# A fused norm, long-convolution and feed-forward kernel: a new model for its static planner, a GpSimd power in the norms, and less combining on TensorE

## The chip, the core and the metric

The kernel runs on one core of a Trainium2 chip. The metric is the device time of one execution in microseconds; lower is better. A core has TensorE (matmuls, "PE" in the profile), VectorE ("DVE"), ScalarE ("ACT"), GpSimd ("POOL") and SyncE ("SP", which here only issues transfers). The program gives each engine its own list of instructions and the semaphores on which it waits for the others.

Times are medians of single executions; a profile shows one execution.

## The reference, cut to what matters

```python
x  = A_q                                        # 2048 rows x 640
h  = x + A(layernorm(x), k, v, shift_k, ssm_k)  # "first norm"; A: kv = shift(k) * v,
                                                #  y = causal FFT convolution of kv with ssm_k, q * y
h2 = h + B(layernorm(h), w_gate, w_up, w_down)  # "second norm"; B: (silu(g) * u) @ w_down, width 1728
# layernorm(x) = (x - mean) / sqrt(var + 1e-5)
```

## The kernel before

The 2048 rows are cut into four blocks of 512 rows. A block's rows lie in four row groups of 128; its 640 columns are worked in two halves. For each block the kernel does: the shift and product k·v (VectorE), forward transforms (TensorE, evicted by ScalarE), products of spectra with those of all earlier blocks (VectorE), inverse transforms (TensorE), the second norm, transposes, and the feed-forward part. The feed-forward matmuls of block j are independent of the convolution of block j+1 and so serve as filler for TensorE while that convolution waits for VectorE and ScalarE.

The order of instructions is not written by hand. The program lists operations with priorities and planned durations. A greedy planner, run when the kernel is built, fixes one order per engine, and the built kernel holds these orders.

```python
# planned durations, us; n = elements per partition
def act_c(n, ptr=False): return 0.17 + 0.000833 * n + (0.09 if ptr else 0)
def dve2(n, psum=False): return 0.15 + 0.00052 * n
def mm_c(n, k=1):        return k * (n / 2400.0 + 0.003)
...
# in the planner: an operation o on engine e, started at t
o.finish = t + o.engs[e]; free[e] = o.finish
for s in o.succ:                                 # hand-off to every consumer: lat = 0.12
    fin = o.finish + (0.0 if o.dma is not None else lat)
...
P.schedule(0.12, dma_model, 1.0)                 # 1.0: when VectorE takes an eviction from ScalarE
```

```python
# both norms end in this; all four row groups at once
if j == 0:      # block 0
    P.op({"act": 0.2}, ... func=ACTF.Sqrt ...)   # square root on ScalarE, then a VectorE reciprocal
else:           # blocks 1 to 3: Newton's method, each o(...) one GpSimd operation on 128x4 numbers
    o(va = src * k1 + eps); o(y = first guess from the bits of va)
    for _ in range(3):
        o(t = y * y); o(t = t * va); o(t = -0.5 * t + 1.5); o(y = t * y)
o(nm = -mean * y)                                # on GpSimd for every block
```

(The two norm snippets are abridged: the arguments of `o` are shown as formulas.)

## Time and profile before

The kernel takes 361.57 us (median of 3, 359.22 to 362.79).

From the page of the kernel before, the span, the busy time of each engine, and two rows of the picture in 40 slices of 9 us (busy tenths of TensorE, and the clock granted to it in tenths):

```profile
span 361.3 us, 5379 instructions
PE 314.9 (87%) x2005; PEld 168.1 (47%) x2024; DVE 225.4 (62%) x366; ACT 203.0 (56%) x319; POOL 68.5 (19%) x147
PE   4697797389999999979999996549999999999993
PEclk9998997559999999999999999558999999999997
```

TensorE is busy 87% of the time, and it is at half clock ("5"; 0.50 in both) in two places: 60-80 us and 227-247 us. Around both it stands again and again.

The table by stage cuts the span at events of the kernel before: start of block 0's feed-forward (75.7), statistics of block 1's second norm ready (140.3), its transposes (152.7), statistics of block 2 (232.9), its transposes (242.9), start of its feed-forward (247.6). Columns: stretch and its length, then the busy time of TensorE, weight loads, VectorE, ScalarE and GpSimd with their counts, granted clock, share of DMA, GB/s.

```profile
core 0: us, PE busy (x) PEld busy (x) DVE busy (x) ACT busy (x) POOL busy (x), PEclk, DMA share, GB/s
0.00:75.70 75.70, 53.50 (x339) 31.57 (x341) 50.26 (x97) 51.14 (x87) 25.08 (x42) 0.87 0.74 244
75.70:140.30 64.60, 63.50 (x398) 31.66 (x403) 50.17 (x79) 43.22 (x66) 12.20 (x24) 0.97 0.30 103
140.30:152.70 12.40, 12.40 (x98) 7.87 (x96) 8.81 (x16) 6.49 (x9) 8.80 (x18) 1.00 0.31 101
152.70:232.90 80.20, 71.83 (x471) 37.26 (x475) 67.94 (x106) 52.47 (x88) 8.92 (x19) 0.96 0.25 85
232.90:242.90 10.00, 3.38 (x23) 1.30 (x22) 6.47 (x13) 6.01 (x11) 6.35 (x15) 0.50 0.19 67
242.90:247.60 4.70, 4.65 (x35) 3.18 (x37) 1.48 (x2) 3.21 (x6) 0.00 (x0) 0.53 0.10 35
```

Between block 2's statistics and its transposes TensorE is busy 3.38 of 10.0 us at half clock (0.50). Between block 1's it is fully busy (12.40 of 12.40 us, clock 1.00).

The GpSimd chain runs from 232.96 to 240.47 us in block 2.

### The profile page before, as it was taken

The numbers are of one execution on the slowest core, as the hardware profiler recorded it, in microseconds if no ns is written. First come the engines' busy times: TensorE is split into PE (matmuls) and PEld (weight loads), VectorE is DVE, ScalarE is ACT, GpSimd is POOL, SyncE is SP. The second block draws the span as 40 slices with busy tenths as digits, with TensorE's granted clock in tenths as the row PEclk, the third lists the DMA queues.
The fourth block names the chain that finished last, engine by engine and source line by source line (L and its number), as shares of the span: only waits on it lengthen the run. The fifth ranks groups of instructions, "written<-read, shape, count | busy, mean of one in ns | idle before, by whom it ended". The sixth has DMA issues, their size and how long they took to land.

```text
span 361.3 us, 5379 instructions
## 1 busy us (share of the span) xinstructions
PE 314.9 (87%) x2005; PEld 168.1 (47%) x2024; DVE 225.4 (62%) x366; ACT 203.0 (56%) x319; POOL 68.5 (19%) x147
## 2 busy tenths in 40 slices
PE   4697797389999999979999996549999999999993
PEld 1374463144435466545445662125444466444561
DVE  1869498486597879578889796955486541122200
ACT  4384988669756745588863257777654503322111
POOL 2504235302502014500240001153100021000000
PEclk9998997559999999999999999558999999999997
DMA  7994558712411531351110135211300101000011
GB/s 224 365 409 148 167 201 214 250 64 109 139 73 43 205 144 39 121 201 36 38 73 2 40 125 164 89 58 37 110 0 10 64 18 38 18 2 0 2 36 37
DMA packets 22013, 37.16 MB, mean 103 GB/s; under 512 B 2616, under 2 KB 17363, under 8 KB 21988
## 3 DMA queue, kind: packets, MB, share of 16 engines
q1 hardware_dynamic: 17524, 20.49, 16.1%
q0 software_dynamic: 3968, 15.98, 13.7%
q10 hardware_dynamic: 496, 0.36, 0.3%
q8 instruction: 16, 0.26, 0.3%
q14 instruction: 9, 0.07, 0.1%
HBM read 22.40 MB, written 2.62 MB: 69 GB/s over the span
## 4 chain that ended last, share of the span: by engine, by line
PE 69%; DMA 9%; ACT 6%; DVE 5%; POOL 5%; issue 4%; ACTq 0%; POOLq 0%; DVEq 0%
PE ps L548 65%; DVE sb L753 4%; PE ps L632 3%; ACT sb L533 3%; DMA sb<-in_B_w_down_dram 2%; PE ps L1067 2%; DMA sb<-in_A_k_dram 2%; DMA sb<-in_A_ssm_k_dram 2%; DMA sb<-in_B_w_gate_dram 2%; ACT sb L894 1%; POOL sb L541 1%; DMA sb<-in_A_v_dram 1%; DMA sb<-in_B_w_up_dram 1%; POOL stt L880 1%; POOL stt L879 1%
## 5 line engine op out<-in xcount | busy, mean ns | idle before, releaser
L548 PE MATMUL ps<-sb 128*128 128x320 bf16 (+3 forms) x1207 | 228.9, 339 | 13.5 <-POOL sb L639 5.1
L753 DVE TENSOR_TENSOR sb<-sb 128x1280 bf16<-128x1280 bf16 (+2 forms) x250 | 161.4, 690 | 44.2 <-ACT sb L533 15.9
L548 PEld LDWEIGHTS ps<-sb 128*128 128x128 bf16 (+2 forms) x1226 | 115.2, 99 | 110.7 <-issue 17.1
L533 ACT ACTIVATE sb<-ps 128x640 bf16<-128x640 f32 (+2 forms) x152 | 106.2, 730 | 91.9 <-PE ps L548 74.0
L548 PE MATMUL ps<-sb,tab 128*64 128x320 bf16 (+2 forms) x622 | 81.2, 326 | 17.4 <-ACT sb L533 11.7
L753 DVE TENSOR_TENSOR sb<-ps,sb 128x1024 bf16<-128x1024 f32 (+3 forms) x44 | 43.9, 1013 | 45.0 <-PE ps L548 39.4
L548 PEld LDWEIGHTS ps<-sb,tab 128*64 128x64 f16 (+2 forms) x622 | 38.2, 105 | 58.9 <-issue 28.0
L1105 ACT ACTIVATE sb<-ps 128x1024 bf16<-128x1024 f32 (+2 forms) x32 | 29.3, 915 | 37.2 <-PE ps L548 37.0
L894 ACT ACTIVATE sb<-sb,stt 128x320 bf16<-128x320 bf16 (+1 forms) x42 | 27.8, 709 | 11.8 <-POOL stt L886 7.5
L536 ACT ACTIVATE sb<-ps 128x640 bf16<-128x640 f32 x24 | 16.5, 702 | 9.4 <-PE ps L548 9.1
L873 POOL TENSOR_SCALAR stt<-stt 128x4 f32<-128x4 f32 x6 | 2.7, 443 | 99.4 <-DVE stt L855 61.1
L632 PE MATMUL ps<-sb 128*128 128x128 bf16 (+1 forms) x96 | 13.2, 233 | 2.5 <-DMA sb<-in_A_ssm_k_dram 2.5
L541 POOL DMA_DIRECT2D sb<-in_A_v_dram x6 | 4.7, 787 | 53.0 <-PE ps L548 53.0
L541 POOL DMA_DIRECT2D sb<-in_A_ssm_k_dram x12 | 7.9, 660 | 33.6 <-PE ps L632 33.5
L851 DVE BATCH_NORM_STATS2 stt<-sb 128x6 f32<-128x320 bf16 x32 | 14.0, 480 | 0.0
L1067 PE MATMUL ps<-sb 128*128 128x128 bf16 x80 | 7.5, 266 | 6.7 <-ACT sb L536 3.5
L913 ACT ACTIVATE sb<-sb,stt 128x640 bf16<-128x640 bf16 x16 | 13.2, 824 | 0.1
L632 PEld LDWEIGHTS ps<-sb 128*128 128x128 bf16 (+1 forms) x96 | 8.6, 117 | 8.3 <-DMA sb<-in_A_ssm_k_dram 3.1
L906 ACT ACTIVATE sb<-sb 128x640 bf16<-128x640 bf16 x16 | 11.8, 734 | 0.1
L534 DVE COPY sb<-ps 128x1280 bf16<-128x1280 bf16 x4 | 3.3, 824 | 12.1 <-PE ps L1067 12.1
L1067 PEld LDWEIGHTS ps<-sb 128*128 128x128 bf16 x80 | 6.4, 122 | 8.6 <-ACT sb L536 4.5
L893 DVE TENSOR_SCALAR sb<-sb,stt 128x640 bf16<-128x640 bf16 x6 | 2.4, 443 | 9.0 <-POOL stt L886 9.0
(30 smaller groups left out, 72.1 us busy)
## 6 DMA issues: line engine op xcount, KB each, us to landing
sb<-sb SPq DMA_DIRECT2D x72, 160.0 KB, 2.2
sb<-in_A_k_dram POOLq DMA_DIRECT2D x6, 560.0 KB, 5.3
out_dram<-sb SPq DMA_DIRECT2D x16, 160.0 KB, 1.8
sb<-cst_den SPq DMA_DIRECT2D x9, 256.0 KB, 5.2
sb<-in_B_w_gate_dram POOLq DMA_DIRECT2D x5, 416.0 KB, 3.6
sb<-in_B_w_up_dram POOLq DMA_DIRECT2D x5, 416.0 KB, 4.2
sb<-in_A_q_dram POOLq DMA_DIRECT2D x3, 640.0 KB, 4.4
sb<-in_A_v_dram POOLq DMA_DIRECT2D x6, 320.0 KB, 4.2
```

The costliest lines, as they stand in the source:

```text
L533: fns = {"act": lambda a: a.activation(out=dst(), in_=src(), func=ACTF.Copy), "dve": lambda v: v.tensor_copy(out=dst(), in_=src())}
L536: fns = {"act": lambda a: a.activation(out=dst(), in_=src(), func=ACTF.Copy, scale=scale), "dve": lambda v: v.tensor_scalar(out=dst(), in0 ...
L541: fns = [(lambda g, d=d, s=s: g.dma_start(d(), s())) for d, s in subs]
L548: return lambda t: t.matmul(o(), l(), r(), start=st, stop=sp)
L632: return t.transpose(B16(pt, b // 2, (b % 2) * CW + d * 128, pr), src, V(IDN, 0, pr, 0, pr))
L753: return lambda v: v.tensor_tensor(out=o(), in0=a(), in1=b_(), op=op)
L851: vec(dve1(CW, False), lambda v: v.bn_stats(st6(l, j, b, c), V(xt, b * D + c * CW, CW)), [(xt, (b, c))], [(ST, ("s", l, j, b, c))], prio, ...
L894: "act": lambda a: a.activation(out=dst(), in_=src(), func=ACTF.Identity, scale=rs(l, j, b), bias=tmv(l, j, 3)[:, b:b + 1])},
L906: P.op({"act": act_c(D) + 0.22}, lambda a, b=b, jt=jt: a.activation(out=V(jt, 0, D), in_=V(xt, b * D, D), func=ACTF.Copy, accum_out=tmv(l, ...
L913: P.op({"act": act_c(D) + 0.3}, lambda a, b=b, jt=jt: a.activation(out=V(jt, 0, D), in_=V(xt, b * D, D), func=ACTF.Square, bias=tmv(l, j, ...
L1067: fns.append(lambda t, k=k, d=d: t.transpose(B16(pt, k, d * 128, 128), V(hn[k], d * 128, 128), V(IDN, 0, 128)))
L1105: P.op({"act": act_c(n)}, lambda a: a.activation(out=dst(), in_=src(), func=ACTF.Silu), rd, wr, -1000, name=f"si{j}{i}")
```

## The change

The intent: plan with durations nearer to the measured ones, and give the plan a TensorE clock that can fall; shorten the norms; take combining work off TensorE where VectorE has time. The diff, cut to its core (the clock rule `pe_end` lowers the planned speed of TensorE by the share of its time that was busy in the plan; its constants, like those of `FRESH`, are planning numbers of the program's):

```diff
+    FRESH = {"pe": 0.22, "act": 0.145, "dve": 0.125, "pool": 0.15, "sp": 0.1}
+    OVERLAP = {"pe": 0.0, "act": 0.105, "dve": 0.085, "pool": 0.0, "sp": 0.0}
...
-                        o.finish = t + o.engs[e]
+                        c = o.engs[e] - self.OVERLAP[e]
+                        o.finish = self.pe_end(t, c) if e == "pe" else t + c
...
-                        fin = o.finish + (0.0 if o.dma is not None else lat)
+                        k = s.deps[o]
+                        if k == 0 or (e == "pe" and "pe" in s.engs):
+                            fin = o.finish
+                        else:
+                            fin = o.finish + max(self.FRESH[x] for x in s.engs)
...
-    RESPE = [True] * 4
+    CMB = [True, False, False, True]      # True: VectorE combines two products before the inverse stage
+    RESPE = [True, True, False, False]    # True: TensorE adds the residual to the feed-forward sum
...
-            return P.op({"pe": mm_c(n, k)}, fns, ...
+            return P.op({"pe": mm_c(n, k) + (0.13 if name.startswith("s2") else 0.03)}, fns, ...
...   # norms: sqrt/reciprocal and the Newton chain are removed
+            vec(0.16, va = src * k1 + eps)
+            P.op({"pool": 0.4}, lambda g: g.tensor_tensor(out=y, in0=va, in1=<-0.5>, op=ALU.pow), ...
+            vec(0.16, nm = -mean * y)
...   # second norm by pairs of row groups
-            (ln_act if LN2A[j] else ln_dve)(1, j, pb + 400)
             for bp in range(2):
+                ln_dve(1, j, pb + 400, range(2 * bp, 2 * bp + 2))
                 ln_bp(j, bp, pb + 400)
...
-        P.schedule(0.12, dma_model, 1.0)
+        P.schedule(dma_model, 0.8)
```

Smaller parts: a GpSimd transfer issue is planned at 0.9 instead of 0.5 us, a freed buffer at 0.14 instead of 0.1 us, one load of block 0 moves from SyncE's queue to ScalarE's. (The lines with `va`, `nm` and `<-0.5>` are abridged.)

More of the change, by code (lines that the diff above doesn't have):

```diff
@@ L42 @@
     ENG = ("pe", "act", "dve", "pool", "sp")
+    FRESH = {"pe": 0.22, "act": 0.145, "dve": 0.125, "pool": 0.15, "sp": 0.1}
+    OVERLAP = {"pe": 0.0, "act": 0.105, "dve": 0.085, "pool": 0.0, "sp": 0.0}
+    WIN = 3.41333
     def __init__(self):
@@ L102, in op, with pe_end, schedule @@
         return o
-    def schedule(self, lat, dma_model, bias):
+    def pe_end(self, t, c):
+        w = self.clock
+        while c > 1e-12:
+            k = int((t + 1.7) // self.WIN)
+            while w["k"] < k:
+                u = w["busy"].get(w["k"], 0.0) / self.WIN
+                if w["s"] == 1.0:
+                    if u < 0.55 and w["k"] > 8:
+                        w["s"] = 0.5
+                elif u >= 0.83:
+                    w["s"] = 1.0
+                w["k"] += 1
+            e = (k + 1) * self.WIN - 1.7
+            if e - t < 1e-9:
+                e += self.WIN
+            d = min(c / w["s"], e - t)
+            w["busy"][k] = w["busy"].get(k, 0.0) + d
+            t += d
+            c -= d * w["s"]
+        return t
+    def schedule(self, dma_model, bias):
+        self.clock = {"k": -1, "s": 1.0, "busy": {}}
         free = {e: 0.0 for e in self.ENG}
@@ L177, in schedule @@
                         if tl.left == 0 and tl.pool is not None:
-                            self.pools[tl.pool].free.append((max(p.finish for p in tl.touch) + 0.1, tl.base, tl.touch))
+                            self.pools[tl.pool].free.append((max(p.finish for p in tl.touch) + 0.14, tl.base, tl.touch))
                     for s in o.succ:
                         s.npred -= 1
-                        fin = o.finish + (0.0 if o.dma is not None else lat)
+                        k = s.deps[o]
[3 more added lines that the diff above has]
+                            fin = o.finish + max(self.FRESH[x] for x in s.engs)
                         s.ready = max(s.ready, fin)
@@ L408, in bass_sequential_preLN__ssm_conv_h3__swiglu_ffn__prompt_kernel @@
     NFB = 14
-    NEWTS = ["pool", "pool"]
-    LN2A = [False, False, False, False]
-    RESPE = [True] * 4
+    CMB = [True, False, False, True]
+    RESPE = [True, True, False, False]
     FM = 1664
@@ L427, in bass_sequential_preLN__ssm_conv_h3__swiglu_ffn__prompt_kernel @@
         tab = es.enter_context(nc.sbuf_tensor("tab", [128, tab_np.shape[1]], f16))
-        stt = es.enter_context(nc.sbuf_tensor("stt", [128, 192 + 32 + 192 + 1], f32))
+        stt = es.enter_context(nc.sbuf_tensor("stt", [128, 192 + 32 + 192 + 8], f32))
         ps = es.enter_context(nc.psum_tensor("ps", [128, 4096], f32))
@@ L541, in dma @@
             fns = [(lambda g, d=d, s=s: g.dma_start(d(), s())) for d, s in subs]
-            return P.op({eng: 0.5 * len(subs)}, fns, reads, writes, prio, after=after, dma=(kb, shuffle), name=name)
+            return P.op({eng: (0.9 if eng == "pool" else 0.5) * len(subs)}, fns, reads, writes, prio, after=after, dma=(kb, shuffle), name=name)
         def pe(fns, n, k, reads, writes, prio, reserve=(), name=""):
-            return P.op({"pe": mm_c(n, k)}, fns, reads, writes, prio, reserve=reserve, name=name)
+            return P.op({"pe": mm_c(n, k) + (0.13 if name.startswith("s2") else 0.03)}, fns, reads, writes, prio, reserve=reserve, name=name)
         def mm(o, l, r, st, sp):
@@ L610, in load_kraw @@
                  (lambda: V(t, 2 * B, B, 0, 64), lambda: dram(A_ssm_k, base + 256 * S, [[S, 64], [1, B]]))],
-                328, [], [(t, 0)], prio, name=f"kraw{j}{c}", eng="pool" if j else ("sp" if c else "act"))
+                328, [], [(t, 0)], prio, name=f"kraw{j}{c}", eng="pool" if j else "act")
         def load_x(j, prio):
@@ L835, in agv @@
             return stt[:, o:o + 8].rearrange("p (b s) -> p b s", b=4)[:, :, 1:2].rearrange("p b s -> p (b s)")
-        def EPS():
-            return stt[:, 416:417]
-        P.op({"pool": 0.1}, lambda g: g.memset(EPS(), LN_EPS), [], [(ST, "eps")], -3000, name="eps")
+        P.op({"pool": 0.1}, lambda g: g.memset(stt[:, 420:424], -0.5), [], [(ST, "half")], -3000, name="half")
         def agm(l, j):
@@ L856, in ln_aggr @@
                 [(ST, ("a", l, j, b))], prio, name=f"ag{l}{j}{b}")
-        def ln_rstd(l, j, prio, two_pass):
-            I32 = dt.int32
-            NEWT = NEWTS[l]
-            va, t, y, nm = (tmv(l, j, i) for i in (0, 1, 2, 3))
-            rd = [(ST, ("ss", l, j, b)) if two_pass else (ST, ("a", l, j, b)) for b in range(4)]
-            c1, c2, c3, c4 = [(ST, ("t", l, j, i)) for i in range(4)]
-            src = va if two_pass else agv(l, j)
-            k1 = 1.0 / D if two_pass else 1.0
-            if j == 0:
-                P.op({"act": 0.2}, lambda a: a.activation(out=t, in_=src, func=ACTF.Sqrt, bias=EPS(), scale=k1), rd + [(ST, "eps")], [c2], prio, name=f"sq{l}")
-                vec(0.16, lambda v: v.reciprocal(out=y, in_=t), [c2], [c3], prio, name=f"rc{l}")
-            else:
-                def o(fn, reads, writes):
-                    P.op({NEWT: 0.3 if NEWT == "pool" else 0.16}, fn, reads, writes, prio, name=f"nr{l}{j}")
-                o(lambda v: v.tensor_scalar(out=va, in0=src, scalar1=k1, scalar2=LN_EPS, op0=ALU.mult, op1=ALU.add), rd, [c1])
-                o(lambda v: v.tensor_scalar(out=y.bitcast(I32), in0=va.bitcast(I32), scalar1=-0.5, scalar2=float(0x5F3759DF), op0=ALU.mult, op1=ALU.add),
-                  [c1], [c3])
-                for _ in range(3):
-                    if NEWT == "pool":
-                        o(lambda v: v.tensor_tensor(out=t, in0=y, in1=y, op=ALU.mult), [c3], [c2])
-                        o(lambda v: v.tensor_tensor(out=t, in0=t, in1=va, op=ALU.mult), [c2, c1], [c2])
-                        o(lambda v: v.tensor_scalar(out=t, in0=t, scalar1=-0.5, scalar2=1.5, op0=ALU.mult, op1=ALU.add), [c2], [c2])
-                        o(lambda v: v.tensor_tensor(out=y, in0=t, in1=y, op=ALU.mult), [c2, c3], [c3])
-                        continue
-                    o(lambda v: v.scalar_tensor_tensor(out=t, in0=y, scalar=-0.5, in1=y, op0=ALU.mult, op1=ALU.mult), [c3], [c2])
-                    o(lambda v: v.tensor_tensor(out=t, in0=t, in1=va, op=ALU.mult), [c2, c1], [c2])
-                    o(lambda v: v.scalar_tensor_tensor(out=y, in0=t, scalar=1.5, in1=y, op0=ALU.add, op1=ALU.mult), [c2, c3], [c3])
-            P.op({NEWT: 0.3 if NEWT == "pool" else 0.16}, lambda v: v.tensor_tensor(out=nm, in0=tmv(l, j, 5), in1=y, op=ALU.mult),
-                 [c3, (ST, ("negm", l, j))], [c4], prio, name=f"nm{l}{j}")
@@ new lines, in ln_rstd @@
+        def ln_rstd(l, j, prio, two_pass, bs):
+            lo, hi = bs[0], bs[-1] + 1
+            va, y, nm, ng = (tmv(l, j, i)[:, lo:hi] for i in (0, 2, 3, 5))
+            if two_pass:
+                src, k1, rd = va, 1.0 / D, [(ST, ("ss", l, j, b)) for b in bs]
+            else:
+                src, k1, rd = agv(l, j)[:, lo:hi], 1.0, [(ST, ("a", l, j, b)) for b in bs]
+            c1, c3, c4 = ([(ST, ("t", l, j, i, b)) for b in bs] for i in (0, 2, 3))
+            vec(0.16, lambda v: v.tensor_scalar(out=va, in0=src, scalar1=k1, scalar2=LN_EPS, op0=ALU.mult, op1=ALU.add), rd, c1, prio, name=f"va{l}{j}")
+            P.op({"pool": 0.4}, lambda g: g.tensor_tensor(out=y, in0=va, in1=stt[:, 420:420 + hi - lo], op=ALU.pow), c1 + [(ST, "half")], c3, prio,
+                 name=f"nr{l}{j}")
+            vec(0.16, lambda v: v.tensor_tensor(out=nm, in0=ng, in1=y, op=ALU.mult), c3 + [(ST, ("negm", l, j, b)) for b in bs], c4, prio,
+                name=f"nm{l}{j}")
@@ L889, in norm @@
         def norm(dst, src, n, l, j, b, reads, writes, prio, name):
-            rd = reads + [(ST, ("negm", l, j)), (ST, ("t", l, j, 2)), (ST, ("t", l, j, 3))]
+            rd = reads + [(ST, ("negm", l, j, b)), (ST, ("t", l, j, 2, b)), (ST, ("t", l, j, 3, b))]
             P.op({"dve": dve4(n), "act": act_c(n) + 0.12}, {
@@ L909, in ln_act @@
             vec(0.16, lambda v: v.tensor_scalar(out=tmv(l, j, 5), in0=tmv(l, j, 4), scalar1=-1.0 / D, scalar2=None, op0=ALU.mult),
-                [(ST, ("sum", l, j, b)) for b in range(4)], [(ST, ("negm", l, j))], prio, name=f"l{l}m{j}")
+                [(ST, ("sum", l, j, b)) for b in range(4)], [(ST, ("negm", l, j, b)) for b in range(4)], prio, name=f"l{l}m{j}")
             for b in range(4):
@@ L914, in ln_act, with ln_dve @@
                     out=V(jt, 0, D), in_=V(xt, b * D, D), func=ACTF.Square, bias=tmv(l, j, 5)[:, b:b + 1], accum_out=tmv(l, j, 0)[:, b:b + 1]),
-                    [(xt, (b, c)) for c in range(2)] + [(ST, ("negm", l, j))], [(jt, 0), (ST, ("ss", l, j, b))], prio, name=f"l{l}v{j}{b}")
-            ln_rstd(l, j, prio, True)
-        def ln_dve(l, j, prio):
-            for b in range(4):
+                    [(xt, (b, c)) for c in range(2)] + [(ST, ("negm", l, j, b))], [(jt, 0), (ST, ("ss", l, j, b))], prio, name=f"l{l}v{j}{b}")
+            ln_rstd(l, j, prio, True, range(4))
+        def ln_dve(l, j, prio, bs):
+            for b in bs:
                 ln_aggr(l, j, b, prio)
-            vec(0.16, lambda v: v.tensor_scalar(out=tmv(l, j, 5), in0=agm(l, j), scalar1=-1.0, scalar2=None, op0=ALU.mult),
-                [(ST, ("a", l, j, b)) for b in range(4)], [(ST, ("negm", l, j))], prio, name=f"l{l}m{j}")
-            ln_rstd(l, j, prio, False)
+            lo, hi = bs[0], bs[-1] + 1
+            vec(0.16, lambda v: v.tensor_scalar(out=tmv(l, j, 5)[:, lo:hi], in0=agm(l, j)[:, lo:hi], scalar1=-1.0, scalar2=None, op0=ALU.mult),
+                [(ST, ("a", l, j, b)) for b in bs], [(ST, ("negm", l, j, b)) for b in bs], prio, name=f"l{l}m{j}")
+            ln_rstd(l, j, prio, False, bs)
         def kv_block(j, c, prio):
@@ L984, in conv_hs @@
             ax = SXt[1, c] if j == 3 else None
+            if CMB[j]:
+                combine((a1, a2), lambda: V2(a1, 0, 640, n, CW), lambda: V2(a2, 0, 640, n, CW), n,
+                        [(a1, i) for i in range(n)], [(a2, i) for i in range(n)], pr, f"{j}{c}{h0}")
             for i, h in enumerate(hs):
@@ L987, in conv_hs @@
                 o_ = i * 640
-                ops_ = [(lambda p0, p1, o_=o_: V(a1, o_, CW, p0, p1), wre), (lambda p0, p1, o_=o_: V(a1, o_ + CW, CW, p0, p1), wneg),
-                        (lambda p0, p1, o_=o_: V(a2, o_, CW, p0, p1), wim), (lambda p0, p1, o_=o_: V(a2, o_ + CW, CW, p0, p1), wim)]
+                if CMB[j]:
+                    ops_ = [(lambda p0, p1, o_=o_: V(a1, o_, CW, p0, p1), wre), (lambda p0, p1, o_=o_: V(a2, o_, CW, p0, p1), wim)]
+                else:
+                    ops_ = [(lambda p0, p1, o_=o_: V(a1, o_, CW, p0, p1), wre), (lambda p0, p1, o_=o_: V(a1, o_ + CW, CW, p0, p1), wneg),
+                            (lambda p0, p1, o_=o_: V(a2, o_, CW, p0, p1), wim), (lambda p0, p1, o_=o_: V(a2, o_ + CW, CW, p0, p1), wim)]
                 cells = [(a1, i), (a2, i)]
@@ L1033, in conv_bp @@
             vec(dve2(2 * CW), tt(hv, hv, lambda: V2(ot, 0, CW, 2, CW), ALU.add), xc2 + [(ot, 0)], xc2, pr, name=f"h{j}{c}{bp}")
-            if not LN2A[j]:
-                for k in range(2):
-                    ln_stats(1, j, bp * 2 + k, c, xt, pr)
+            for k in range(2):
+                ln_stats(1, j, bp * 2 + k, c, xt, pr)
         def conv_c(j, c):
@@ L1192, in dma_model @@
                 dmafree[0] = s + 0.55
-                return s + 2.2
+                return s + 2.3
             s = max(issued + (1.2 if o.eng == "pool" else 0.8), link[0])
```

## The prediction

> **What bounds the kernel now.** The page gives TensorE 314.9 us busy of 361.3 (87%), VectorE 62%, ScalarE 56%; the chain of waits is 69% TensorE. The time is TensorE work at full clock, plus the extra of work at half clock, plus idle. The table of 5-us windows locates the losses. Half clock: 60-80 us (12.6 us busy, about 6 extra) and 227-247 us (10 busy, 5 extra). Idle: the load (8 us before 15 us), 55-80 us (9.5), 215-250 us (12), the tail (6). The two mid-kernel stages lose 16-17 us each; those the change can get. [...]
>
> **Why they stall (timeline by engine).** At 232.9 us block 2's second norm has its statistics; then 15 tiny GpSimd operations (128x4; 0.19 to 0.85 us each) run until 240.5 us: 7.6 us for a reciprocal root. Transposes follow at 242.9; the filler, block 1's feed-forward, is used up by 217. [...] the trace shows one operation at 0.2 us with VectorE idle and 0.8 beside it. In block 0 the reciprocal is ready at 62.5 us, but the last GpSimd multiply waits in its queue behind a w_down transfer until 66.6; transposes begin at 70.9.
>
> **What changes.**
> - The chain becomes VectorE, one GpSimd power, VectorE, by row pairs. Estimate from the 128x4 times: 0.2 + 0.8 + 0.2 us, 1.5 with hand-offs, instead of 7.6. Block 2: 6 us of wait and 1.5 of half clock. Block 0: the multiply leaves the GpSimd queue, but the power is in it behind weight transfers: 0-5 us, I take 3. Blocks 1 and 3 hide under feed-forward matmuls: 0.
> - Square root leaves ScalarE, with one or two table loads of 1.28 us, one in the chain at 39.7 us: 1 us.
> - TensorE: block 3's inverse stage drops 32 of 224 64x320 matmuls (20.2 us in all, so 2.9); residual adds of blocks 2 and 3 drop 16 matmuls of 128x320 (0.151 us each, 2.4). Both lie after 247 us, where TensorE is nearly always busy: 5 us.
> - Added: VectorE combines in block 3 (8 of 0.48 us) and additions for copies at 8 outputs; VectorE is some 55% busy there: nearly free.
> - The new order, from truer latencies: fewer stalls on ScalarE evictions (19 waits, 14.8 us). It is greedy, and VectorE stays over 80% busy from 165 to 240 us: only 3 us.
>
> Sum 5 + 7.5 + 3 + 1 + 3, about 19 us.
>
> **Prediction: 343 us, 8 in 10 between 333 and 354. Faster by over 2%: 0.87; within 2%: 0.11; slower: 0.02.**
>
> **What shows it.** TensorE busy near 300; the stage 225-250 loses under 10 us, and block 2's gap from last statistics to transposes falls from 10 us to about 4; no square root on ScalarE; 55-80 us still has a slow clock, but shorter; block 3's feed-forward, the last 47 us, shrinks by only 1.2.
>
> **What would make it wrong.** The power taking several us; the power stuck behind transfers on the GpSimd queue in block 0 or 2; the new order using up the filler earlier, moving the hole rather than closing it; or the order closing both holes (325-330 us).

(Two passages are cut from it. The one in the first paragraph gave a rule for when the clock falls, and concluded that a stall is paid twice. The traces show the half clock (0.50 in 60-80 and 227-247 us) but not that rule: see "The clock" below. The one in the second paragraph gave a reason why GpSimd is slower beside VectorE; measured are only the durations that follow it (0.2 us with VectorE idle, 0.8 beside it). No term of the sum is cut, it is still about 19 us; the 1.5 us of half clock in block 2's 7.5 were my estimate, which no trace shows apart.)

## More of the kernel before

The timeline of the kernel before (start, duration, engine, line, operation, output<-input, count, and in brackets the idle time before and what ended it):

```profile
140.96 6.17 DVE L753 TENSOR_TENSOR sb<-sb 128x1280 bf16<-128x1280 bf16 x9
150.24 0.80 DVE L893 TENSOR_SCALAR sb<-sb,stt 128x640 bf16<-128x640 bf16 x2 [3.12 <-POOL stt L886]
...
232.96 0.65 POOL L873 TENSOR_SCALAR stt<-stt 128x4 f32<-128x4 f32 x1 [12.23 <-DVE stt L855]
233.69 0.39 POOL L874 TENSOR_SCALAR stt<-stt 128x4 int32<-128x4 int32 x1
...
240.27 0.20 POOL L886 TENSOR_TENSOR stt<-stt 128x4 f32<-128x4 f32 x1
242.87 2.31 PE L1067 MATMUL ps<-sb 128*128 128x128 bf16 x20 [2.78 <-ACT sb L536]
```

## The result and the profile after

The kernel after takes 330.18 us (median of 4, 329.36 to 331.60); the kernel before took 361.88 us in the same rounds. A ratio is the mean time of one kernel's fast runs over that of the other's of the same rounds, so it is not quite the ratio of the medians; here it is 0.914 (95% interval 0.909 to 0.919). The direction was right. The gain is 31.7 us where 19 were predicted, and the time lies just below the range.

From the page of the kernel after:

```profile
span 327.8 us, 5229 instructions
PE 299.1 (91%) x1956; PEld 162.0 (49%) x1976; DVE 235.3 (72%) x406; ACT 197.5 (60%) x310; POOL 47.9 (15%) x67
PE   3899785489999999999999999999989999999992
PEclk9999999579999999999999999999999999999998
```

The half clock is left in one place (0.60 in 54-66 us). Of the 33.5 us between the spans, 15.8 are TensorE busy time (314.9 - 299.1) and 17.7 are TensorE idle time (46.4 before, 28.7 after, each span less busy).

The table by stage of the kernel after, cut at the same events, so that the lines answer to those shown of before:

```profile
0.00:66.30 66.30, 48.88 (x326) 29.77 (x328) 47.39 (x100) 50.94 (x88) 27.82 (x42) 0.93 0.82 268
66.30:122.90 56.60, 55.17 (x352) 27.11 (x358) 49.18 (x78) 40.42 (x60) 7.30 (x10) 0.97 0.37 126
122.90:128.30 5.40, 4.95 (x37) 3.18 (x36) 5.20 (x14) 4.48 (x7) 1.70 (x2) 1.00 0.02 5
128.30:207.30 79.00, 78.51 (x544) 43.23 (x550) 75.50 (x121) 53.95 (x85) 5.69 (x7) 1.00 0.27 91
207.30:212.30 5.00, 4.95 (x39) 2.92 (x38) 4.41 (x15) 3.81 (x6) 1.74 (x2) 1.00 0.28 103
212.30:216.00 3.70, 3.56 (x44) 2.85 (x46) 2.49 (x5) 2.92 (x4) 0.00 (x0) 1.00 0.24 86
```

Line by line the stages shrink by 9.4, 8.0, 7.0, 1.2, 5.0 and 1.0 us; the rest of the kernel, 113.7 us before and 111.8 after, gives 1.9. Two readings matter. The lines that shrink most are those of block 0 and block 1, where I had booked 4 us and nothing. For block 1 this is mostly filler that moved: its two lines hold 15.8 us less TensorE work than before (107 matmuls fewer), the three lines of block 2 hold 98 matmuls more. And block 2's convolution, fourth line, hardly got shorter, but it holds 78.5 us of TensorE work instead of 71.8 and 75.5 us of VectorE work instead of 67.9: the filler now lasts to its end.

The timeline of the kernel after, for the places shown of before:

```profile
123.01 1.70 POOL L894 TENSOR_TENSOR stt<-stt 128x2 f32<-128x2 f32 x2 [2.77 <-DVE stt L932]
124.95 8.68 DVE L783 TENSOR_TENSOR sb<-sb 128x1280 bf16<-128x1280 bf16 x13
...
207.53 1.74 POOL L894 TENSOR_TENSOR stt<-stt 128x2 f32<-128x2 f32 x2 [17.98 <-DVE stt L932]
212.26 1.32 PE L1083 MATMUL ps<-sb 128*128 128x128 bf16 x20
```

Two powers in 1.7 us, with small VectorE operations around them, replace a chain of 7.5 (block 2) and 9.9 us (block 1, 140.26 to 150.20). VectorE no longer stands behind the norm in block 1, and block 2's transposes come with no idle time before them.

### The profile page after: what moved, and what is told of

The parts are those of the page before. It is cut to its first block, busy times and chain, and to the rows that moved or that the text cites. A ratio compares the mean times of both kernels' runs of the same rounds, so it can differ in the third digit from the quotient of the medians.

```text
span 327.8 us, 5229 instructions
## 1 busy us (share of the span) xinstructions
PE 299.1 (91%) x1956; PEld 162.0 (49%) x1976; DVE 235.3 (72%) x406; ACT 197.5 (60%) x310; POOL 47.9 (15%) x67
## 3 DMA queue, kind: packets, MB, share of 16 engines
q1 hardware_dynamic: 17172, 20.16, 17.7%
## 4 chain that ended last, share of the span: by engine, by line
PE 69%; DVE 10%; ACT 8%; DMA 5%; issue 3%; POOL 3%; ACTq 0%; POOLq 0%; DVEq 0%
PE ps L578 65%; DVE sb L783 9%; ACT sb L563 4%; PE ps L662 3%; ACT sb L904 2%; DMA sb<-in_A_ssm_k_dram 2%; DMA sb<-in_A_k_dram 2%; DMA sb<-in_B_w_gate_dram 2%; POOL stt L894 1%; PE ps L1083 1%; POOL sb L571 1%; ACT sb L923 1%; ACT sb L1121 1%; ACT sb L916 1%; DVE stt L878 0%
## 5 line engine op out<-in xcount | busy, mean ns | idle before, releaser
L578 PE MATMUL ps<-sb 128*128 128x320 bf16 (+2 forms) x1192 | 225.0, 338 | 8.3 <-DMA sb<-in_A_shift_k_dram 2.4
L783 DVE TENSOR_TENSOR sb<-sb 128x1280 bf16<-128x1280 bf16 (+2 forms) x258 | 165.6, 683 | 30.1 <-DMA sb<-in_A_k_dram 10.2
L578 PEld LDWEIGHTS ps<-sb 128*128 128x128 bf16 (+3 forms) x1212 | 113.2, 98 | 102.3 <-issue 18.2
L563 ACT ACTIVATE sb<-ps 128x640 bf16<-128x640 f32 (+2 forms) x146 | 101.7, 737 | 44.3 <-PE ps L578 34.9
L783 DVE TENSOR_TENSOR sb<-ps,sb 128x1024 bf16<-128x1024 f32 (+3 forms) x52 | 50.5, 982 | 45.4 <-PE ps L578 42.4
L578 PE MATMUL ps<-sb,tab 128*64 128x320 bf16 (+2 forms) x588 | 70.1, 309 | 7.1 <-DMA sb<-sb 3.0
L578 PEld LDWEIGHTS ps<-sb,tab 128*64 128x64 f16 (+2 forms) x588 | 35.4, 102 | 41.7 <-issue 15.2
L894 POOL TENSOR_TENSOR stt<-stt 128x2 f32<-128x2 f32 (+1 forms) x12 | 12.4, 1039 | 97.2 <-DVE stt L893 76.4
L662 PE MATMUL ps<-sb 128*128 128x128 bf16 (+1 forms) x96 | 13.6, 240 | 2.8 <-DMA sb<-in_A_ssm_k_dram 2.8
L571 POOL DMA_DIRECT2D sb<-in_A_k_dram x6 | 5.9, 987 | 11.7 <-DVE sb L783 11.7
L896 DVE TENSOR_TENSOR stt<-stt 128x2 f32<-128x2 f32 (+1 forms) x12 | 1.9, 160 | 6.8 <-POOL stt L894 6.7
```

Of the source, the lines that this page charges most:

```text
L563: fns = {"act": lambda a: a.activation(out=dst(), in_=src(), func=ACTF.Copy), "dve": lambda v: v.tensor_copy(out=dst(), in_=src())}
L571: fns = [(lambda g, d=d, s=s: g.dma_start(d(), s())) for d, s in subs]
L578: return lambda t: t.matmul(o(), l(), r(), start=st, stop=sp)
L662: return t.transpose(B16(pt, b // 2, (b % 2) * CW + d * 128, pr), src, V(IDN, 0, pr, 0, pr))
L783: return lambda v: v.tensor_tensor(out=o(), in0=a(), in1=b_(), op=op)
L894: P.op({"pool": 0.4}, lambda g: g.tensor_tensor(out=y, in0=va, in1=stt[:, 420:420 + hi - lo], op=ALU.pow), c1 + [(ST, "half")], c3, prio, ...
```

## The experiments

The question is where the 13 us beyond the prediction came from. Theory "operations": the time comes from what was removed (the chain, the square root, TensorE work), and the order is worth little; that is my prediction. Rival "order": the truer plan paces the work, and the operations matter little. "Against after" below is (ratio - 0.914) x 362 us, which takes out the small drift of the kernel before (its medians were 361.4 to 362.8 us on four different chips).

All runs are correct and were timed in 3 rounds:

| run | median us | ratio to before | against after, us |
|---|---|---|---|
| kernel after | 330.2 | 0.914 | 0 |
| order_only | 350.3 | 0.968 | 19.3 |
| ops_only | 356.6 | 0.986 | 25.9 |
| slow_norm | 344.4 | 0.952 | 13.9 |
| before_pow | 359.9 | 0.993 | 28.6 |
| cmb_old | 334.5 | 0.926 | 4.2 |
| no_clock | 335.2 | 0.926 | 4.5 |
| no_overlap | 351.1 | 0.971 | 20.5 |
| no_fresh | 335.9 | 0.931 | 6.1 |
| norm_old | 351.8 | 0.971 | 20.7 |
| scaled_pe | 337.9 | 0.933 | 6.9 |
| wd_late | 331.6 | 0.915 | 0.5 |
| wd_pe104 | 331.3 | 0.915 | 0.2 |
| norm_dve | 341.7 | 0.942 | 10.2 |
| norm1_old | 335.7 | 0.927 | 4.7 |
| norm2_old | 341.9 | 0.944 | 10.6 |
| whole | 334.1 | 0.922 | 2.9 |
| bias10 | 331.3 | 0.915 | 0.5 |
| bias06 | 333.4 | 0.923 | 3.1 |

Half-widths of the 95% intervals are 0.004 to 0.009 of the ratio. The last column compares two such ratios, so its half-width is about 2.4 to 3.7 us (estimate from both intervals); differences below that mean nothing.

### Order alone, operations alone

`order_only` has the planner of after and the operations of before; `ops_only` the reverse.

```diff
# order_only, on the kernel before: FRESH, OVERLAP, pe_end, planned costs and schedule(dma_model, 0.8) as in the change;
#             norms, CMB, RESPE, queues as before
# ops_only, on the kernel after:
-        P.schedule(dma_model, 0.8)
+        P.schedule(0.12, dma_model, 1.0)   # and the old finish, hand-off and cost lines
```

> All operations of the kernel before (long GpSimd chain, residual adds and inverse-stage combines on TensorE), planned with the new latencies and clock rule. Theory 'operations' (the prediction's sum: order worth 3 us): about 355-359 us. Rival theory 'order' (the plan's truer durations pace the feed-forward filler so that block 2's end no longer finds TensorE without work): 336-345 us, and the half-clock stretch at 227-247 us shrinks or is gone.

> All operations of the kernel after, planned with the old latencies and without the clock rule. Theory 'operations': about 345 us (16 of the 19 us predicted). Theory 'order': 348-356 us, with a TensorE hole before block 2's transposes still there.

Alone, the order gains about 12 us (ratio 0.968) and the operations 5 us (0.986). The product of the ratios, 0.954, would be 17 us; together they give 31. Both theories fall: most of the surplus over 17 us exists only when both are there. In `ops_only` the gap before block 2's transposes is still there (TensorE busy 6.0 of 15 us in 225-240 us at a clock of 0.60). In `order_only` it is smaller but there (transposes at 230.1 us, with 3.31 us idle before them). How the two halves combine can be read from the last filler before block 2's transposes: it ended 25.8 us ahead of them in the kernel before, 23.0 in `ops_only`, 9.2 in `order_only`; in the kernel after filler runs right up to them (it ends at 212.21 us, they start at 212.26). The new order makes the filler last longer, the short norm brings the transposes forward, and only both together close the hole.

### The norm in a frozen order

Two runs change only how long the second norm of blocks 1 to 3 takes and leave every order as planned. `slow_norm` puts the old chain into the kernel after, `before_pow` puts the power into the kernel before.

```diff
# slow_norm (after; planned duration stays 0.4, so the order does not move)
-            P.op({"pool": 0.4}, <power>, ...)
+            P.op({"pool": 0.4}, chain if l == 1 and j > 0 and lo == 0 else <power>, ...)   # 13 dependent operations
# before_pow (before; the 13 planned operations keep their places, one is emitted)
+            if j > 0 and l == 1:
+                mine[1].fns = <power>
+                for q in mine[2:]: q.skip = True
```

> The kernel after with its order frozen; only in the second norm of blocks 1 to 3 the first pair's power is replaced by the old chain of 13 dependent GpSimd operations, some 5-7 us long. Theory 'operations': the norm is on the path, so 6 to 7.5 us slower than the kernel after (336-338 us). Theory 'order': feed-forward matmuls now last until about 216 us while block 2's transposes were at 212, so most of the delay is hidden: 0 to 3 us slower (330-333 us).

> The kernel before with its order frozen; in the second norm of blocks 1 to 3 the chain after the variance becomes one GpSimd power on all four row groups (one power instead of 13 operations). Theory 'operations': block 2 gains 5 to 7 us, blocks 1 and 3 little: 354-357 us. Theory 'order' expects the same here, as the filler has run out in this order: it is the pair with slow_norm that tells them apart.

Neither number was expected. In the new order three chains of 3.5 to 4.3 us, one in each of blocks 1 to 3, stand for three powers of 0.7 to 0.9 us. That is 9.3 us more GpSimd time, and it costs 14 us. Taking the chains out of the old order gains only 2.6 us. The timeline of `slow_norm` at block 1, where I had expected the norm to hide under filler:

```profile
128.59 2.71 PE L584 MATMUL ps<-sb 128*128 128x320 bf16 x18
134.66 2.26 PE L1097 MATMUL ps<-sb 128*128 128x128 bf16 x20 [3.36 <-ACT sb L569]
136.71 2.52 PE L584 MATMUL ps<-sb 128*128 128x320 bf16 x12
```

The filler is there, right behind the transposes (third line), but TensorE's order puts the transposes first, so it stands 3.36 us. The 12 filler matmuls did not step over the waiting transposes. The loss repeats in all three blocks (transposes later than in the kernel after by 6.4, 11.0 and 14.8 us). Not all of this is the chain's: block 1's statistics, before the first chain, already came 3.5 us later in this execution (125.87 against 122.39 us), although both kernels do the same up to there. From statistics to transposes the three blocks lost 2.9, 3.0 and 2.2 us. The rest came behind the transposes, where the clock fell (0.89 in 135-150 us, against 1.00 in the kernel after).

The timeline of `before_pow` at block 2:

```profile
233.67 1.23 POOL L894 TENSOR_TENSOR stt<-stt 128x4 f32<-128x4 f32 x1
...
236.63 0.83 ACT L924 ACTIVATE sb<-sb,stt 128x640 bf16<-128x640 bf16 x1
...
238.04 1.72 ACT L905 ACTIVATE sb<-sb,stt 128x640 bf16<-128x640 bf16 x2
...
240.87 2.31 PE L1078 MATMUL ps<-sb 128*128 128x128 bf16 x20 [0.80 <-ACT sb L539]
```

The norm's factors are ready at about 235.2 us instead of 240.5. But ScalarE's order, planned for the long chain, has sums of squares for block 3's first norm in front of the normalising operations (L905), which start at 238.04. The transposes come only 2 us earlier. So in a static order an operation's duration and its place belong together: here the shortened operation paid only when the order was planned again, and the lengthened one cost 14 us for 9.3.

### Which part of the plan

```diff
# no_clock
-  o.finish = self.pe_end(t, c) if e == "pe" else t + c
+  o.finish = t + c
# no_overlap
-  OVERLAP = {"pe": 0.0, "act": 0.105, "dve": 0.085, ...
+  OVERLAP = {"pe": 0.0, "act": 0.0, "dve": 0.0, ...
# no_fresh
-  fin = o.finish + max(self.FRESH[x] for x in s.engs)   # and the 0 for pure order
+  fin = o.finish + (0.0 if o.dma is not None else 0.12)
# scaled_pe: no_overlap, and
-  {"pe": mm_c(n, k) + (0.13 if name.startswith("s2") else 0.03)}
+  {"pe": 1.16 * (mm_c(n, k) + (0.13 if name.startswith("s2") else 0.03))}
```

> The kernel after with the clock rule left out of the plan (TensorE always planned at full clock), the new latencies kept. Theory 'truer latencies do it': within 3 us of the kernel after (328-333 us), since the greedy planner sees the clock only as a duration of a few stretches. Rival 'the clock rule does it': 8 us or more slower (338 us or more), with half-clock stretches back.

> The kernel after with one number of the plan undone: ScalarE and VectorE operations are planned with their full time again, not 0.105 and 0.085 us less, so the plan thinks these two engines slower than they are. Theory 'pacing' (the plan must have the ratio of TensorE to VectorE right, or it uses up feed-forward matmuls too early): 340-352 us with VectorE idle in 90-200 us and the hole before block 2's transposes back. Rival 'hand-off latencies do it': within 4 us of the kernel after.

> The kernel after with the hand-off latency between engines planned as one number (0.12 us) for every consumer again, in place of 0.22 for TensorE, 0.145, 0.125 and 0.15 for the others and 0 for pure order. Theory 'pacing': within 4 us of the kernel after (328-335 us). Rival 'hand-off latencies do it': 8 us or more slower.

One number carries the plan. Without OVERLAP 20.5 us are lost; without the clock rule or the hand-offs 4 to 6, a little more than expected and far from the 8 of the rivals. What OVERLAP stands for can be read in the timeline of the kernel before:

```profile
57.09 2.97 ACT L533 ACTIVATE sb<-ps 128x640 bf16<-128x640 f32 x5
60.66 1.30 ACT L533 ACTIVATE sb<-ps 128x640 bf16<-128x640 f32 x2 [0.60 <-PE ps L548]
62.28 0.70 ACT L533 ACTIVATE sb<-ps 128x640 bf16<-128x640 f32 x1
...
222.35 5.89 DVE L753 TENSOR_TENSOR sb<-sb 128x1280 bf16<-128x1280 bf16 x8 [2.95 <-DMA sb<-in_A_v_dram]
```

One such eviction lasts 0.70 us, but two take 1.30 and five 2.97: the next starts before the last has ended, by about 0.10 us in the second line and 0.13 us each in the first. The old plan had 0.703 us for each, exact for a single one and too long in a row. VectorE behaves the same (last line: 8 products of 0.83 us took 5.89 us in a row, so about 0.10 us each).

The old plan thus took ScalarE and VectorE for slower than they are, beside a TensorE planned at full clock throughout (measured: 0.50 in 60-80 and 227-247 us). It expects the convolution to wait for them and fills the time with feed-forward matmuls, which are then missing at the convolution's end. In `no_overlap` block 2's convolution took 91 us instead of 79, and the last filler ended at 213 us, 17 us before the transposes. (How long VectorE waited for TensorE in all does not tell the plans apart: 55.5 us here, 49.2 in the kernel after, but 50.5 in the kernel before.) The timeline of `no_overlap`, the last filler first:

```profile
211.84 1.35 PE L578 MATMUL ps<-sb 128*128 128x320 bf16 x8
...
218.17 0.46 PE L578 MATMUL ps<-sb,tab 128*64 128x320 bf16 x4 [0.66 <-ACT sb L563]
222.41 2.98 PE L578 MATMUL ps<-sb,tab 128*128 128x320 bf16 x12 [3.78 <-ACT sb L916]
230.65 1.25 PE L1083 MATMUL ps<-sb 128*128 128x128 bf16 x10 [4.19 <-ACT sb L904]
```

This is the hole of the kernel before again, with the short norm in place. Is it the ratio between the engines or the durations as such? `scaled_pe` keeps the wrong durations and makes TensorE dearer by the same factor.

> As the run that plans ScalarE and VectorE too slow, but TensorE work is planned 1.16 times dearer as well, so the ratio between the engines is right again while every planned time is too long (the plan ends at 362 us). Theory 'pacing, the ratio counts': most of the 21 us come back, 329-340 us, and the hole before block 2's transposes is gone. Rival 'absolute durations count' (against transfers and hand-offs): it stays at 346-352 us.

It brings back 13.6 of the 20.5 us (337.9 us), as the theory of the ratio expected, and block 2's transposes move from 230.7 to 216.3 us, with filler right up to them. About 7 us do not come back; transfers and hand-offs, whose planned times were not scaled, are a possible cause that I did not test.

### Which part of the norm

`norm_old` is the kernel after with both norms as before, planned for with the new planner. The other three split it.

```diff
# norm_old:  ln_rstd of the kernel before, whole blocks; all else as after
# norm_dve:  norm_old with
-    NEWTS = ["pool", "pool"]
+    NEWTS = ["dve", "dve"]        # the chain on VectorE
# norm1_old: after, first norm only as before;   norm2_old: after, second norm only as before
# whole:     after, with
-                ln_dve(1, j, pb + 400, range(2 * bp, 2 * bp + 2))   # inside the loop over pairs
+            ln_dve(1, j, pb + 400, range(4))                        # ahead of it
```

> The kernel after in everything (planner, combines, residual adds) except the norms, which are those of the kernel before: square root on ScalarE in block 0, the GpSimd chain of 15 operations in blocks 1 to 3, one norm for all four row groups; planned for with the same new latencies. If the norm is worth what is left over between the other runs (about 350 of the order alone, minus some 4 for the TensorE work, against 330), it is 344-347 us. The prediction's term for the norm and the square root was 11.5 us, which would be 341-342 us. If replanning can hide the long chain, 331-336 us.

> As the run with the old norms and all else new, but the chain of blocks 1 to 3 runs on VectorE (13 small operations of some 0.16 us) instead of 15 on GpSimd. Theory 'GpSimd starves beside VectorE': most of the 21 us come back, 331-338 us. Rival 'a chain for all four row groups is what costs, whatever the engine': 345-352 us.

> The kernel after, with only the first norm as before (square root on ScalarE in block 0, GpSimd chain in blocks 1 to 3). The first norm is needed late in its block's convolution, so I expect 0 to 3 us slower than the kernel after (330-333 us); if the chain in the GpSimd queue holds up the loads of k and v behind it, 5 us or more.

> The kernel after, with only the second norm as before (square root in block 0, GpSimd chain in blocks 1 to 3, for four row groups at once). If the second norm is the one on the path, it carries most of the 21 us: 343-351 us.

> The kernel after with its one GpSimd power, but the second norm for all four row groups at once, not by pairs. If the short chain is what counts, within 4 us of the kernel after (329-334 us); if the pairs are, 338 us or more.

In the new plan the norms are worth 20.7 us, not the 11.5 I had given them: 10.6 for the second alone, 4.7 for the first alone (0 to 3 expected). The row pairs are worth 2.9 us, which is within the noise. With the old norms the smaller TensorE work shows nothing at all (`norm_old` 351.8 us, `order_only` 350.3 us).

Part of the reason is seen at block 1 in the timeline of `norm_old`:

```profile
128.90 7.47 POOL L905 TENSOR_SCALAR stt<-stt 128x4 f32<-128x4 f32 x1 [2.66 <-DVE stt L887]
129.16 8.95 DVE L785 TENSOR_TENSOR sb<-sb 128x640 bf16<-128x640 bf16 x14
136.46 0.77 POOL L906 TENSOR_SCALAR stt<-stt 128x4 int32<-128x4 int32 x1
...
143.72 0.45 DVE L925 TENSOR_SCALAR sb<-sb,stt 128x640 bf16<-128x640 bf16 x1 [5.61 <-POOL stt L918]
```

The first operation of the chain lasts 7.47 us while VectorE runs 14 products without a break; then VectorE stands 5.61 us for the chain. In the second norms of the kernel before, `order_only` and `norm_old`, the chain of 15 took 4.1 us in block 3 with an idle VectorE, and 7.5 to 14.8 us in blocks 1 and 2 beside a busy one. In block 1 it took 9.9 us in the kernel before, 10.1 in `order_only` and 14.8 in `norm_old`; 1.3 to 2.3 us of that are transfers that GpSimd issues in between. The same 128x4 operation (L879 in block 2 of the kernel before) took 0.78 us at 237.09 us, beside VectorE products, and 0.20 us at 239.43 us with VectorE idle. By these durations the old chain is longer beside a busy VectorE, for a reason that no run shows; in `norm_old` the chain then hands the loss back to VectorE (the 5.61 us). That a truer order does this in general is not shown: in `order_only`, with the same planner and the same norms, the chain of block 1 was hardly longer than before (10.1 and 9.9 us), and VectorE stood at most 1.8 us at a time for any of the chains.

How much is the engine's doing? On VectorE (`norm_dve`) the same arithmetic brings back 10.5 of 20.7 us, less than I expected. The other half is not explained by the engine. Candidates are the square root in block 0, which stays, the whole-block form (2.9 us by `whole`), and the extra small operations on VectorE; I did not separate them.

### TensorE work, and the GpSimd queue

```diff
# cmb_old
-    CMB = [True, False, False, True]
-    RESPE = [True, True, False, False]
+    CMB = [True, False, False, False]
+    RESPE = [True, True, True, True]
# wd_late: transfers of w_down wait for block 0's second power, so they queue behind it
-  after=chain[-2:-1] or [kv_last[0, 0]]
+  after=(chain[-2:-1] or [kv_last[0, 0]]) + ([nr_last[1, 0]] if nm in ("wd", "wdl") else [])
# wd_pe104: wd_late, and TensorE work planned 1.04 times dearer
```

> The kernel after, but block 3's inverse stage combines on TensorE again (32 matmuls more) and blocks 2 and 3 add their residual on TensorE again (16 matmuls more). The plan's milestones up to block 2's transposes are unchanged by it. Theory 'TensorE work lies on the path after 215 us' (the prediction's term): 4 to 6 us slower than the kernel after, 334-336 us. Rival, 'VectorE is as loaded as TensorE there and pays for what TensorE saves': within 2 us of the kernel after.

> The kernel after, with one dependency more: the transfers of w_down wait for block 0's second power, so they cannot stand before it in the GpSimd queue. If that queue is what delays block 0's second norm (power ready to run at 52.9 us, run at 58.7 us), 3 to 6 us faster than the kernel after: 324-327 us. If something else ends last there, no change (329-331 us).

> As the run with the late w_down transfers, and TensorE work planned 4% dearer (the trace of the kernel after shows 299 us busy, the plan has 287). If the plan still uses the feed-forward filler too early, another 1-4 us faster; if the pace is right already, within 2 us of the run with the late w_down transfers.

The TensorE work put back costs 4.2 us, near the 5 predicted, but see the next section for what 4 us can mean. By stages the gain is smaller: from the start of block 2's feed-forward to the end the span took 113.7 us before and 111.8 after.

`wd_late` did what it was made for: block 0's second power ran at 57.5 instead of 58.7 us and its feed-forward began at 64.3 instead of 66.3 us. The gain was lost by block 2, whose feed-forward began at 220.8 instead of 216.0 us. The kernel ends where the kernel after does, and so does `wd_pe104`. No version I made beats the kernel after.

### What a reshuffled plan costs

Nearly every part undone cost 3 to 6 us, which made me suspect the reshuffling itself.

```diff
-        P.schedule(dma_model, 0.8)
+        P.schedule(dma_model, 1.0)    # bias10; 0.6 in bias06
```

> The kernel after, with the one number that decides whether ScalarE or VectorE evicts a tile set back from 0.8 to 1.0 us, as before. No operation is added or removed, three evictions move from VectorE to ScalarE. If the small losses of the other runs belong to the parts they undo, this is within 1.5 us of the kernel after (329-332 us). If any reshuffling of the tuned plan costs some us, it is 333-337 us.

> The same number set to 0.6 us. The plan's own end is 312.8 us against 313.1 us for the kernel after, so by the plan nothing is lost. Within 1.5 us of the kernel after if the small losses belong to the parts; 333-337 us if any reshuffling costs some us; below 329 us would beat both kernels.

A tie-breaking number moved to either side costs 0.5 and 3.1 us. The first is noise; the second, twice the 1.5 us allowed to "the parts", is just beyond its half-width of 2.9 us. So a new order may cost some 3 us by itself, and the 3 to 6 us of `no_clock`, `no_fresh`, `whole`, `norm1_old` and `cmb_old` cannot be put down to their parts with confidence. The 20 us of OVERLAP, the norms together and the second norm stand well clear of it.

## Why the prediction was wrong, point by point

- **The step that failed: "The new order, from truer latencies: ... only 3 us."** The order alone is worth 12 us with the old operations and 26 us with the new ones (`ops_only` against after). I counted the eviction waits on TensorE and took VectorE's load as fixed. I did not ask when the plan spends its filler. I had the sign of it in hand: "used up by 217" stood in my text as a fact of the kernel, while it is a choice of the plan.
- **The norm's term was mis-sized, and adding terms was wrong.** I gave norms and square root 11.5 us; in the new plan they are worth 20.7 us, in the old frozen order the second norm's power is worth 2.6 us (blocks 1 to 3). The sum treated order and operations as independent: 17 us if they were, 31 measured.
- **"Blocks 1 and 3 hide under feed-forward matmuls: 0."** Wrong for block 1: TensorE was busy there, so I called it hidden; but VectorE stood 3.12 us behind the chain, and with the chain back in the new order (`slow_norm`) statistics to transposes took 2.9 us longer. The line of the table shrank by more, from 12.4 to 5.4 us, but most of that is filler that moved to block 2 (TensorE busy 12.40 and 4.95 us). For block 3 `slow_norm` says the same (2.2 us longer).
- **Block 2: right in size, partly by luck.** I gave 7.5 us; the two stages from statistics to feed-forward shrank by 6.0 us, and the gap from statistics to transposes fell from 10.0 to 5.0 us (about 4 predicted). The stage 225-250 us lost almost nothing instead of "under 10". But I gave this to the short norm alone, and alone it brought 2.6 us (`before_pow`): the order had to bring the filler.
- **Block 0: too low.** 4 us for norm and square root were booked; its feed-forward starts 9.4 us earlier. No run splits the 9.4 us. The power was stuck behind transfers as foreseen, for 5.8 us (52.9 to 58.7), a little over the 0 to 5 allowed, but freeing it (`wd_late`) gained nothing in the end.
- **TensorE work: about right, not clear of the noise.** Busy time fell to 299.1 us ("near 300"), but by 15.8 us, of which the removed matmuls are only 5.3 by my own estimate (2.9 + 2.4); the rest I put down to the half clock, which is not shown apart. The run that puts the work back lost 4.2 us against 5, the stages show 1.9 us.
- **Added VectorE work nearly free, last feed-forward 1.2 us shorter: right.** VectorE's busy time grew by 9.9 us with no stage after block 2 suffering by more than 0.7 us; from the start of block 3's feed-forward to the end took 53.0 us before and 52.0 after.
- **The clock.** My text took a rule for when the clock falls as given; the traces do not show it. What they show: in the kernel before the clock fell to 0.50 at about 59.6 and 226.9 us; in 56-60 and 223-227 us TensorE was busy 1.8 and 1.5 of 4 us, and its longest gap there was 2.32 us. What makes it fall, these runs do not tell. Planning for the clock was worth about the 4.5 us of `no_clock`, which a mere reshuffling might cost too.

I named "the order closing both holes (325-330 us)" as a way to be wrong and gave it too little weight. It closed one: 55-70 us still has a clock of 0.55.

## What to carry to other kernels

Where engines follow a fixed order, a busy TensorE does not mean that a delay is hidden: look at which other engine stands in its queue (here VectorE, 3.12 us in block 1 of the kernel before), and at whether the filler in reach is spent in time. Plan with the cost of an operation in a row, not alone (a ScalarE eviction 0.59 us in a row of five, 0.70 alone): here the ratio between the engines decided how fast the filler was used up. And do not add the gain of a shorter operation to the gain of a better order: replan, measure both together, and treat a few microseconds after any replanning as noise until a neutral change has shown how large it is.

## What else the traces show

- One GpSimd 128x4 operation took 7.47 us in `norm_old`, beside an unbroken run of 14 VectorE products (8.95 us, about 0.64 us each), so for as long as some 11 of them. One took 4.46 us in `norm2_old`; what VectorE did beside that one was not looked at. In block 3 of the kernel before, with VectorE idle, the same two operations took 0.19 us each. Seen twice, not reproduced on purpose; spans on GpSimd are rough in this profile.
- An elementwise power on GpSimd took 1.50 us on average for 128x4 and 0.81 us for 128x2 (kernel after, 4 and 8 of them, VectorE busy 72% of the span), where other 128x4 operations of the kernel before took 0.2 to 0.85 us.
- A table load on ScalarE took 1.283 us, three times in the kernel before and twice in the kernel after. At 39.66 us in the kernel before, ScalarE was busy up to the load and went on 0.02 us after it, so no loss beside the load shows there.
